# A new order for the opening of an attention + Fourier-mixing kernel, with query sums on VectorE and scaling ahead of the turn

## The chip, the cores and the metric

The kernel runs on one core of a Trainium2 chip. The metric is the device time of one execution in microseconds (us). A core has five engines that work side by side and wait for each other through semaphores: TensorE (PE in the profile; its weight loads are listed apart as PEld), VectorE (DVE), ScalarE (ACT), GpSimd (POOL) and SyncE (SP), which here only issues transfers. Each engine takes its own instructions strictly in the order in which the program issues them. A transfer (DMA) is issued by one of the engines' queues and then runs on its own.

## What is computed

```python
def _attn_ref(q, k, v):                      # q, k, v: (8 batches, 8 heads, 576 rows, 64)
    q_s = np.exp(q - np.max(q, axis=-1, keepdims=True))
    q_s = q_s / (np.sum(q_s, axis=-1, keepdims=True) + 1e-09)
    k_s = np.exp(k - np.max(k, axis=2, keepdims=True))
    k_s = k_s / (np.sum(k_s, axis=2, keepdims=True) + 1e-09)
    kv = np.einsum('bhsd,bhse->bhde', k_s, v)
    return np.einsum('bhsd,bhde->bhse', q_s, kv)

def _moe_ref(x, w_ch1, w_ch2):               # x: (8, 576, 512), the heads side by side
    X = np.fft.fft(np.fft.fft(x, axis=1), axis=2)
    u = x + np.real(X)
    mu, var = mean and variance of u over the last axis
    un = (u - mu) / np.sqrt(var + 1e-06)
    return u + np.maximum(un @ w_ch1, 0.0) @ w_ch2      # 512 x 2048 and 2048 x 512
```

All of it is float32. The two feed-forward weights arrive as 64-bit numbers and are turned into float32 on the chip, in part by steps called `c0 hi`, `c0 shift`, `c0 sign`, `c0 lo`, `c0 add` for the first block of columns.

## The kernel before

The eight batches go through three stages: attention, the two Fourier transforms with the layer normalisation, and the two feed-forward matmuls. Each batch has 576 rows: 512 of its own in four tiles of 128 and 64 that are left over. The left-over rows of batches 0 and 1 share one tile, called `t` here. A program of steps with times is written out in the kernel: every step is a pair (time, function), the main function sorts all pairs by time (the end of the printed code) and calls them in that order under `manual_schedule`. The times are labels for sorting. What counts is the order that results on each engine and the waits that data bring.

The change touches the opening: the work on batch 0 ahead of the first feed-forward matmul. Its steps and their order stand in the string `OPENING` (L86), and a few warm-up matmuls, which compute nothing that is used, in `WARM` (L85). `opening()` (L575) gives each name its function. The steps, in the order of the data:

- Loads. `loads_first()` (L246) gives the first transfers to SP's queue: four key tiles, the query tiles A and B in one transfer (`queries(0)`), half of the values (L285, L286), the query tiles C and D (`queries(1)`), the shared tile's four blocks of 32 rows (`shared()`, L271), the other half of the values, and then four single rows that take the first place in each of those four blocks (`shared_firsts()`, L274). A small exponential on ScalarE (`table`) has its function table loaded early.
- Keys. `k00` to `k03` are four tiles of the transposed keys of batch 0. `max` (VectorE, L529) finds the maximum of a row, `exp` (ScalarE) the exponential and its sum, `turn` and `four` transpose it on TensorE and copy it on ScalarE; `last` and `fifth` (L548) do the same for the left-over rows. `k0 inverse` (L550 to L552) inverts the sums, `k00 kv` to `k03 kv` multiply with the values, and `k0 scale0` and `k0 scale1` (L561) scale the result. The names with `k1` are the same for batch 1.
- Queries. A, B, C and D are the four tiles of batch 0: A is (column half 0, unit 0), B (1, 1), C (0, 1) and D (1, 0). `max` (VectorE, L805), `less` (GpSimd, L810; on VectorE for `t`) and `exp` (ScalarE, L814) make the exponential in place. `turn` and `copy` transpose it into a tile `qT` from a pool of two buffers (L832). `ones` (L876) multiplies the transposed tile with a matrix of ones, which gives the sum of each head; `inverse` (L887) inverts it on VectorE; `kv` (L884) multiplies with the keys-times-values, and `out` (L899) scales the product on its way from PSUM to the tile `x`. For `t` the sum, inverse and scaling come ahead of the turn (`t inverse`, `t normal`, on VectorE).
- Folding. `t turn`, `t copy`, `t fold`, `t join`, `t kv`, `t parts`, `t folds` bring the shared rows into the transform. `tokens0` to `tokens3` (L945) are sums and differences of pairs of outputs: 0 and 2 of A's with C's, 1 and 3 of D's with B's. `columns`, `by`, `again` (L951 to L965) fold the columns likewise. `b0` to `b4` (`block()`) are the transform along the columns; `m0` and `m1` (`mix_own()`, L1061) that along the rows, with the `sums` at L1042, for the column halves 0 and 1.
- Normalisation. `s00` to `s11` (L1075) are the statistics of the four mixed tiles, `root0` and `root1` the square roots (L1079), `normal` the normalised tile, `turn` (L1105) and `laid` (L1114) its transpose into the tile that the feed-forward reads.
- Feed-forward. The first matmul takes its first columns in two halves (`half(0)` and `half(1)`, L1169). `half(0)` reads the tiles 00 and 01 and `half(1)` the tiles 10 and 11. Next come the matmuls of L1160, which read the converted weights (L377).

Time `first = 46.9` (L1588) places the feed-forward in the list.

Of the kernel before, what the change touches and what calls it, by code (L numbers as in the profile page):

```python
# [46 lines left out]
P = 128  # L47
# [37 lines left out]
WARM = (3, 3), (24.7, 6), (41.9, 2), (43.45, 1), (44.5, 1)  # L85
OPENING = """  # L86
4.30 k00 max, 5.10 k00 exp, 5.50 k01 max, 6.05 k00 turn, 6.30 k01 exp, 6.65 k02 max, 7.06 k00 four,
7.25 k01 turn, 7.56 k02 exp, 7.75 k03 max, 8.32 k01 four, 8.51 k02 turn, 8.82 k03 exp, 8.90 A max, 9.50 B max,
9.58 k02 four, 9.65 A less, 9.77 k0 last, 10.10 k0 inverse, 10.27 k03 turn, 10.42 k0 fifth, 10.69 B less,
10.80 A exp, 11.20 k00 kv, 11.30 k03 four, 11.84 B exp, 11.85 A turn, 12.20 C max, 12.30 k01 kv, 12.45 A copy,  # L90
12.80 D max, 12.95 B turn, 12.95 C less, 13.40 A ones, 13.55 B copy, 13.99 D less, 14.10 C exp, 14.20 k02 kv,
14.35 A inverse, 14.85 C turn, 15.00 t max, 15.14 D exp, 15.30 k03 kv, 15.75 t less, 15.95 D turn,
16.35 k0 scale0, 16.40 B ones, 16.47 t exp, 16.80 k0 scale1, 17.14 t inverse, 17.25 B kv, 17.99 B inverse,
18.22 A kv, 18.35 C copy, 18.39 t normal, 19.01 B out, 19.19 t turn, 19.32 D copy, 19.63 k10 max, 19.69 C ones,
19.84 t copy, 20.30 A out, 20.43 k10 exp, 20.49 C kv, 20.92 C inverse, 21.39 t fold, 21.46 D ones,
22.09 t join, 22.26 D kv, 22.51 D inverse, 22.91 C out, 23.31 t kv, 23.53 D out, 24.15 tokens0, 24.21 k10 turn,
24.36 t parts, 24.77 tokens1, 25.39 columns0, 25.46 k10 four, 25.75 columns1, 26.23 by1, 26.59 by0,
26.80 c0 hi, 26.95 t folds, 27.45 c0 lo, 27.70 again0, 28.00 again1, 28.50 tokens3, 28.60 b0 times,
29.12 tokens2, 29.58 b1 times, 29.74 columns3, 29.80 b0 copies, 30.10 columns2, 30.56 b4 times, 30.58 by2,
30.78 b1 copies, 30.94 by3, 31.42 again2, 31.72 again3, 31.76 b4 copies, 32.22 k12 max, 32.32 b2 times,  # L100
32.89 c0 shift, 33.02 k12 exp, 33.30 b3 times, 33.59 c0 sign, 33.78 b2 copies, 34.19 k13 max, 34.28 k12 turn,
34.31 c0 add, 34.50 b3 copies, 34.86 k11 max, 35.05 k13 exp, 35.20 m0 times, 35.81 k12 four, 36.10 k13 turn,
36.31 m0 copy, 36.55 m1 times, 36.66 k11 exp, 36.81 m0 sums, 37.42 k13 four, 37.61 k1 last, 37.71 m0 add0,
37.92 m1 copy, 38.07 k11 turn, 38.27 k1 fifth, 38.39 m0 add1, 38.42 m1 sums, 38.77 k11 four, 38.92 k10 kv,
39.22 s00, 39.27 roots, 39.67 k11 kv, 39.69 m1 add1, 39.97 s01, 40.42 k12 kv, 40.87 root0, 40.99 m1 add0,
41.17 k13 kv, 41.67 scales0, 41.87 s11, 42.02 normal01, 42.62 s10, 42.77 turn01, 43.37 normal00, 43.52 root1,
43.87 scales1, 43.89 normal11, 43.95 laid01, 44.02 turn00, 44.22 normal10, 44.77 laid00, 44.87 turn10,
45.47 turn11, 45.62 laid10, 46.22 laid11, 53.00 k1 inverse, 53.30 k1 scale0, 53.60 k1 scale1"""
# [28 lines left out]
class _Block:  # L137
    def __init__(self, ctx, tc, q, kT, v, w1, w2, ft, cd, out):
# [38 lines left out]
        self.ones = c.tile([P, NR, H], F32, name="ones")  # L177
        nc.gpsimd.memset(self.ones[:], 0.0)
        for h in range(2):
            nc.gpsimd.memset(self.ones[64 * h:64 * h + 64].rearrange("p r h -> p (r h)")[:, h::H + 2], 1.0)  # L180

# [31 lines left out]
        self.unused = None  # L213
# [32 lines left out]
    def loads_first(self, fetch):  # L246
# [20 lines left out]
        def shared():  # L267
            flat = self.q[b:b + 2].rearrange("b s n -> (b s) n")
            for i in range(4):
                a = i * S // 2 + P  # L270
                load(tail[i * Q:(i + 1) * Q], flat[a:a + Q])  # L271

        def shared_firsts():
            load(tail[0:P:Q], self.q[b:b + 2].rearrange("b s n -> (b s) n")[::S // 2])  # L274
# [5 lines left out]
        def keys(r):  # L280
            load(ks[r], self.kT[b, r * P:(r + 1) * P, :])
# [10 lines left out]
        def second(r):  # L292
# [6 lines left out]
        order = [lambda: nc.gpsimd.memset(v[0:64, 4, :], 0.0), table, *(lambda r=r: keys(r) for r in range(NR)), lambda: queries(0),  # L299
                 lambda: values(0), lambda: queries(1), shared, lambda: values(2), shared_firsts, self.tables,  # L300
# [214 lines left out]
    def first_keys(self, b):  # L515
# [4 lines left out]
        copy, box, top = nc.vector.tensor_copy if b == 0 else nc.scalar.copy, {}, {}  # L520
# [26 lines left out]
        def fifth():  # L547
            copy(self.fifth[64:], box["last"][64:])  # L548
# [26 lines left out]
    def opening(self, fetch, converted):  # L575


        V, G = self.nc.vector, self.nc.gpsimd
# [14 lines left out]
        named("t max,t less,t exp", self.q_exp_spread(shared, V))  # L593
        named("t inverse,t normal", self.q_inverse(shared, V, V))
# [3 lines left out]
        for n, it in own.items():  # L598
            named(f"{n} max,{n} less,{n} exp", self.q_exp_spread(it))
            named(f"{n} turn,{n} copy", self.q_turn(it))  # L600
            named(f"{n} ones,{n} kv,{n} inverse,{n} out", self.q_times_kv(it))
# [12 lines left out]
        steps["roots"] = self.roots_next  # L614
        for i in range(1):
# [182 lines left out]
    def q_exp_spread(self, it, e=None):  # L798
# [885 lines left out]
```

## Time and profile before

| what | value |
|---|---|
| time, three runs | 1070.05, 1070.17, 1070.81 us; median 1070.17 |
| the profiled execution | 1070.52 us, of which the profile's span is 1068.70 us |
| TensorE busy | 1057.0 us (99% of the span) |
| TensorE weight loads (beside matmuls) | 921.2 us (86%) |
| VectorE busy | 699.5 us (65%) |
| ScalarE, GpSimd busy | 403.5 us (38%), 376.5 us (35%) |
| chain of work that ended last | TensorE 86%, VectorE 3%, ScalarE 2% |
| transfers | 236.04 MB, mean 221 GB/s |

The profile records one execution. A busy share is an average over the whole span. In the first of 40 slices of it (26.7 us each) TensorE is busy for eight tenths and VectorE for six tenths, and in the last slice TensorE for eight tenths; in the slices between them TensorE stands at nine tenths or more. The granted TensorE clock is at nine tenths or more in all slices. A line of a group names the source line (L1105), the engine, the operation, what it writes and reads with tile names, the shapes, how often, the busy time, the mean of one in nanoseconds, and the idle time of the engine just ahead with the work that ended it. A line of a timeline gives start and length in us and then the same, with the idle time in brackets. The chain of waits follows the work that ended last backwards, from each instruction to the one that released it.

### The profile page before, as it was taken

Reading aid. Unit: us, or ns where it says so; the run is one execution under the profiler, and the core shown is the slowest. Engines: PE = TensorE matmul, PEld = TensorE weight load, DVE = VectorE, ACT = ScalarE, POOL = GpSimd, SP = SyncE. Lnnn points to the kernel's source line nnn. Section 1 sums busy time; section 2 is a strip of 40 time slices with the busy share of each in tenths; the row PEclk is TensorE's granted clock in tenths of the full one; section 3 lists DMA queues with packets and bytes.
Section 4 is the critical chain, followed back from the end, with each engine's and each line's share of the span. In section 5 each row is a group of like instructions: output and inputs, shape, how many; then the busy total and the mean of one; then the engine's idle time right before and its main releaser. Section 6 shows DMA issues by size and latency. Waiting matters only on the chain.

```text
span 1068.7 us, 16982 instructions
## 1 busy us (share of the span) xinstructions
PE 1057.0 (99%) x6394; PEld 921.2 (86%) x6394; DVE 699.5 (65%) x1350; ACT 403.5 (38%) x953; POOL 376.5 (35%) x317
## 2 busy tenths in 40 slices
PE   8999999999999999999999999999999999999998
PEld 7744556988898899889988999889988998899897
DVE  6897887684455874677556765678457745674563
ACT  5675534632245215521453234521552132231210
POOL 3262220265412743454515542374336350000000
PEclk9999999999999999999999999999999999999999
DMA  8697478648976576645755576557644575576464
GB/s 278 225 305 244 174 247 295 210 161 281 337 258 209 180 254 233 226 176 202 269 181 193 197 247 223 187 196 257 223 167 158 201 253 178 197 257 223 170 220 145
DMA packets 113546, 236.04 MB, mean 221 GB/s; under 512 B 23272, under 2 KB 74856, under 8 KB 102840
## 3 DMA queue, kind: packets, MB, share of 16 engines
q1 hardware_dynamic: 113096, 234.42, 64.3%
q8 instruction: 51, 0.84, 0.3%
q10 hardware_dynamic: 288, 0.26, 0.1%
q14 instruction: 31, 0.25, 0.1%
q0 software_dynamic: 80, 0.26, 0.1%
HBM read 199.79 MB, written 39.06 MB: 223 GB/s over the span
## 4 chain that ended last, share of the span: by engine, by line
PE 86%; DVE 3%; ACT 2%; issue 0%; ACTq 0%; DVEq 0%
PE bb L1244 15%; PE bb L1371 10%; PE bc L1244 10%; PE ba L1244 10%; PE bc L1371 7%; PE ba L1371 7%; PE bb L1341 5%; PE acc L716 3%; PE acc L884 2%; PE bc L1181 2%; PE bb L1460 2%; PE acc L997 2%; PE acc L1000 2%; PE acc L1025 2%; PE bc L1460 1%; PE ba L1460 1%
## 5 line engine op out<-in xcount | busy, mean ns | idle before, releaser
L1244 PE MATMUL bb<-unT,big 128*128 128x256 f32 x768 | 184.4, 380 | 0.8 <-DVE u L1214 0.8
L1244 PEld LDWEIGHTS bb<-unT,big 128*128 128x128 f32 x768 | 142.5, 190 | 20.3 <-DVE u L1214 2.3
L1256 ACT ACTIVATE big<-big 128x512 f32<-128x512 f32 x96 | 60.4, 629 | 194.8 <-DVE big L1255 194.3
L1244 PE MATMUL ba<-unT,big 128*128 128x256 f32 x512 | 123.8, 379 | 0.0
L1244 PE MATMUL bc<-unT,big 128*128 128x256 f32 x512 | 123.5, 379 | 0.0
L1214 DVE TENSOR_TENSOR u<-bb,s 128x512 f32<-128x512 f32 x66 | 45.6, 690 | 105.9 <-PE bb L1244 83.0
L383 POOL TENSOR_TENSOR big<-big 128x512 f32<-128x512 f32 x24 | 30.5, 1269 | 226.6 <-ACT big L1256 226.6
L1244 PEld LDWEIGHTS bc<-unT,big 128*128 128x128 f32 x512 | 94.7, 190 | 12.5 <-DVE big L1255 1.0
L1371 PE MATMUL bb<-big 128*128 128x128 f32 x848 | 105.1, 275 | 0.3 <-DVE u L1378 0.3
L1244 PEld LDWEIGHTS ba<-unT,big 128*128 128x128 f32 x512 | 94.4, 190 | 12.2 <-issue 0.5
L1371 PEld LDWEIGHTS bb<-big 128*128 128x128 f32 x848 | 99.6, 192 | 0.5 <-DVE u L1378 0.4
L1321 POOL TENSOR_TENSOR x<-x,big 128x512 f32<-128x512 f32 x45 | 57.7, 1296 | 62.7 <-issue 32.9
L1371 PE MATMUL ba<-big 128*128 128x128 f32 x640 | 79.6, 275 | 0.0
L766 ACT ACTIVATE q<-q,qm 128x64 f32<-128x64 f32 x248 | 67.1, 338 | 31.2 <-DVE qm L760 24.7
L1371 PEld LDWEIGHTS ba<-big 128*128 128x128 f32 x640 | 76.3, 192 | 1.2
L1317 DVE TENSOR_TENSOR big<-big 128x512 f32<-128x512 f32 x98 | 76.3, 818 | 0.0
L1341 PE MATMUL bb<-big 128*128 128x256 f32 x256 | 58.7, 381 | 0.0
L1378 DVE TENSOR_TENSOR u<-bb,s 128x256 f32<-128x256 f32 x40 | 16.8, 421 | 63.9 <-PE bb L1371 60.6
L1255 DVE TENSOR_TENSOR big<-bc,u 128x512 f32<-128x512 f32 x64 | 44.0, 687 | 21.8 <-PE bc L1244 21.0
L1120 POOL TENSOR_TENSOR unT<-unT 128x512 f32<-128x512 f32 x8 | 14.2, 1771 | 123.0 <-DVE unT L1120 100.8
L1341 PEld LDWEIGHTS bb<-big 128*128 128x128 f32 x256 | 48.2, 190 | 8.0 <-DVE big L1255 1.1
L1371 PE MATMUL bc<-big 128*128 128x128 f32 x416 | 51.5, 275 | 0.0
(265 smaller groups left out, 2022.4 us busy)
## 6 DMA issues: line engine op xcount, KB each, us to landing
big<-w2d SPq DMA_DIRECT2D x67, 1024.0 KB, 4.8
big<-w1s SPq DMA_DIRECT2D x64, 896.0 KB, 4.9
big<-w2s SPq DMA_DIRECT2D x16, 1024.0 KB, 6.3
big<-in_w_dram SPq DMA_DIRECT2D x21, 512.0 KB, 6.4
w2d<-big SPq DMA_DIRECT2D x42, 256.0 KB, 5.4
q<-in_q_dram SPq DMA_DIRECT2D x28, 256.0 KB, 6.1
k<-in_kT_dram SPq DMA_DIRECT2D x24, 288.0 KB, 5.5
v<-in_v_dram SPq DMA_DIRECT2D x24, 256.0 KB, 4.7
```

The costliest lines, as they stand in the source:

```text
L383: e1.tensor_tensor(out=to(4), in0=at(2), in1=at(3), op=ALU.add)
L716: nc.tensor.matmul(pk, lhsT=ks[:, c, :], rhs=v[:, c, :], start=(c == 0), stop=(c == NC - 1))
L766: nc.scalar.activation(q[:, h, :], q[:, h, :], ACT.Exp, bias=m[:, h:h + 1])
L1214: plus = lambda t: V.tensor_tensor(out=temp(t), in0=box["bb"][:], in1=box["s1"][:], op=ALU.add)
L1244: nc.tensor.matmul(bank()[:, i, :], lhsT=w[:, WA_AT[m], k * P:(k + 1) * P], rhs=self.unT[g][:, B_AT[m], k, :], start=first and i == 0 and ...
L1255: steps = [(0, lambda: V.tensor_tensor(out=hp(i), in0=bank()[:], in1=u()[:], op=ALU.add)), (0.8, lambda: nc.scalar.activation(hp(i), hp(i) ...
L1256: (0.8, lambda: nc.scalar.activation(hp(i), hp(i), ACT.Relu))]
L1317: e.tensor_tensor(out=to(o), in0=to(x), in1=to(y), op=op)
L1321: E.tensor_tensor(out=x, in0=x, in1=tile(m), op=ALU.add)
L1341: nc.tensor.matmul(box[name][:, i, :], lhsT=h[p][:, A_AT[m], i * P:(i + 1) * P], rhs=self.stream[n][:, p, :], start=p == 0 and (m != 1 or ...
L1371: nc.tensor.matmul(box[place[n]][:, i, :], lhsT=own(m)(A_AT[n])[:, f, :], rhs=w[:, r // 2, r % 2 * P:r % 2 * P + P], start=first and f == ...
L1460: nc.tensor.matmul(bank()[:, i, :], lhsT=h[p][:, A_AT[m], i * P:(i + 1) * P], rhs=w[:, p, :], start=first and i == 0 and p == 0, stop=p == ...
```

## The change

It has five parts.

1. Sums and scaling of the queries. The tile `ones`, its 16 matmuls and the four inverses that follow are gone. Five steps `sum` on VectorE (`reduce_sum`, one for each of t, A, B, C, D) run on the exponentials before the turn. Two steps invert them together: `inverse1` those of t and C, `inverse2` those of D, A and B. The tiles t, C and D are scaled before the turn by GpSimd (`normal`). A and B are scaled by VectorE at `out` as before. The `out` of C and D is a plain copy on ScalarE.
2. Loads. The four block loads of `shared()` are issued by ScalarE's queue ahead of `table`. The load of the four first rows, `firsts`, is issued by ScalarE's queue after the second key exponential, no longer by SP.
3. Engines. `t less` goes from VectorE to GpSimd, `k0 fifth` from VectorE to ScalarE.
4. Places. For batch 0 `qT` has its own places in the weights' tile `w1sb`, where before two buffers took turns. The products of A, B and C go to named PSUM banks. The token sums read the products of C and D straight from PSUM.
5. Order. `OPENING` and `WARM` are new. The half `m1` is mixed before `m0`, and the tiles 11 and 10 are normalised, turned and laid before 01 and 00. `first` is 47.6. `half(0)` still reads 00 and 01.

```diff
-WARM = (3, 3), (24.7, 6), (41.9, 2), (43.45, 1), (44.5, 1)
+WARM = (3, 3), (24.33, 6), (41.46, 1), (44.02, 1)
 OPENING = """
...
+4.10 k00 max, 4.90 k00 exp, 5.25 k01 max, 5.90 k00 turn, 6.05 k01 exp, 6.07 firsts, 6.70 k02 max,
+7.00 k00 four, 7.05 k01 turn, 7.50 k02 exp, 7.75 k03 max, 8.37 k01 four, 8.50 k02 turn, 8.87 k03 exp,
+9.00 B max, 9.60 t max, 9.74 k02 four, 9.75 B less, 9.87 k0 last, 10.20 A max, 10.39 k03 turn, 10.57 k0 fifth,
+10.79 t less, 11.07 B exp, 11.22 k00 kv, 11.57 k03 four, 11.72 B sum, 11.83 A less, 12.07 t exp, 12.32 C max,
+12.34 B turn, 12.79 k01 kv, 12.92 t sum, 12.98 A exp, 13.07 C less, 13.48 B copy, 13.52 D max, 13.91 A turn,
+14.12 k0 inverse, 14.22 C exp, 14.36 k02 kv, 14.47 A sum, 14.47 D less, 14.72 A copy, 15.07 C sum, 15.62 D exp,
+15.71 k03 kv, 15.81 inverse1, 16.27 D sum, 16.31 t normal, 17.06 k0 scale0, 17.36 C normal, 17.46 t turn,
+17.56 k0 scale1, 18.06 B kv, 18.16 t copy, 18.41 inverse2, 18.81 t fold, 18.96 C turn, 19.41 A kv, 19.53 B out,
+19.53 D normal, 19.66 C copy, 20.15 k10 max, 20.34 C kv, 20.82 A out, 20.95 k10 exp, 21.24 D turn,
+21.58 t join, 21.94 D copy, 21.95 k10 turn, 22.13 tokens0, 22.55 k10 four, 22.62 D kv, 22.75 tokens2,
+23.05 C out, 23.37 columns0, 23.52 t kv, 23.77 D out, 23.77 tokens1, 24.39 tokens3, 24.57 t parts,
...
+34.35 k11 four, 34.47 m1 times, 34.85 k13 exp, 35.57 m0 times,
...
+41.24 k12 kv, 41.32 normal11, 41.85 s01, 42.36 turn11, 42.71 s00, 42.96 k13 kv, 43.57 normal10, 43.66 root0,
+44.07 scales0, 44.22 turn10, 44.27 laid11, 44.42 normal01, 44.89 normal00, 44.97 laid10, 45.17 turn01,
+45.77 turn00, 45.92 laid01, 46.52 laid00, 53.00 k1 inverse, 53.30 k1 scale0, 53.60 k1 scale1"""
...
             for i in range(4):
                 a = i * S // 2 + P
-                load(tail[i * Q:(i + 1) * Q], flat[a:a + Q])
-
-        def shared_firsts():
-            load(tail[0:P:Q], self.q[b:b + 2].rearrange("b s n -> (b s) n")[::S // 2])
+                nc.scalar.dma_start(tail[i * Q:(i + 1) * Q], flat[a:a + Q])
...
         def fifth():
-            copy(self.fifth[64:], box["last"][64:])
+            nc.scalar.copy(self.fifth[64:], box["last"][64:])
...
-        named("t max,t less,t exp", self.q_exp_spread(shared, V))
-        named("t inverse,t normal", self.q_inverse(shared, V, V))
+        named("t max,t less,t exp", self.q_exp_spread(shared))
+        sums = self.small.tile([P, 5, H], F32, tag="sums", name="sums", bufs=1)
+        firsts = {"t": shared, **{n: own[n] for n in "CDAB"}}
+        heads = {n: self.live[it][0].rearrange("p (h d) -> p h d", h=H) for n, it in firsts.items()}
+        spread = {n: sums[:, i].unsqueeze(2).to_broadcast([P, H, DH]) for i, n in enumerate(firsts)}
+        for i, n in enumerate(firsts):
+            steps[f"{n} sum"] = lambda i=i, n=n: V.reduce_sum(sums[:, i], heads[n], axis=AX.X)
+            if n in "tCD":
+                steps[f"{n} normal"] = lambda n=n: G.tensor_tensor(out=heads[n], in0=heads[n], in1=spread[n], op=ALU.mult)
+            else:
+                self.live[own[n]].append(spread[n])
+
+        def inverse(s):
+            V.tensor_scalar(out=sums[:, s], in0=sums[:, s], scalar1=ATT_EPS, scalar2=None, op0=ALU.add)
+            V.reciprocal(sums[:, s], sums[:, s])
+
+        for i, s in enumerate((slice(0, 2), slice(2, 5))):
+            steps[f"inverse{i + 1}"] = lambda s=s: inverse(s)
...
+        steps["firsts"] = lambda: nc.scalar.dma_start(self.at_start[3][0:P:Q], rows)
...
-            (e or nc.gpsimd).tensor_tensor(out=heads(), in0=heads(), in1=m, op=ALU.add)
+            nc.gpsimd.tensor_tensor(out=heads(), in0=heads(), in1=m, op=ALU.add)
...
-            qT = self.work.tile([P, NR, P], F32, tag="qT", name="qT", bufs=2)
-            self.nc.scalar.copy(qT[:], pt[:] if c == u else pt[:, :, ::-1])
+            if b == 0:
+                qT = self.w1sb[:, 1 + c + 2 * u, :].rearrange("p (r n) -> p r n", n=P)
+            else:
+                qT = self.work.tile([P, NR, P], F32, tag="qT", name="qT", bufs=2)[:]
+            self.nc.scalar.copy(qT, pt[:] if c == u else pt[:, :, ::-1])
...
-        return [(0, ones), (0, times), (1, inverse), (1.3, out)] if b == 0 else [(0, times), (1.3, out)]
+        return [(0, times), (1.3, out)]
...
-                e.tensor_tensor(out=eo[i][:, 0:D], in0=self.xpart(b, i % 2, 0), in1=self.xpart(b, i % 2, 1), op=op)
+                x, y = ((self.px.get((i % 2, u)) if b == 0 else None) for u in range(2))
+                x, y = (self.xpart(b, i % 2, u) if z is None else z for u, z in enumerate((x, y)))
+                e.tensor_tensor(out=eo[i][:, 0:D], in0=x, in1=y, op=op)
...
-    first, second, both = 46.9, 56, 77
+    first, second, both = 47.6, 56, 77
```

In the changed program the lines are shifted: the query maxima are at L815, `less` at L820, the sums at L591, the scalings of t, C and D at L593, the token sums at L953, the mixed sums at L1050, the turn of the normalised tiles at L1113 and the halves of the first feed-forward matmul at L1177.

## The prediction

> **What bounds the kernel now.** I read the busy time by stretches first, then TensorE's waits after the opening, then the timelines. Columns of the first: stretch in us, its length, busy time of PE, PEld, DVE, ACT and POOL, clock, DMA share, GB/s.
>
> ```profile
> 12.00:16.00 4.00, 3.79 (x35) 3.71 (x34) 1.81 (x5) 2.33 (x4) 2.04 (x2) 1.00 0.59 128
> 16.00:30.00 14.00, 13.02 (x104) 12.19 (x103) 12.82 (x35) 5.89 (x11) 1.48 (x3) 1.00 1.03 344
> ...
> 48.80:1068.70 1019.90, 1014.00 (x6092) 883.21 (x6090) 662.91 (x1260) 375.09 (x888) 361.93 (x282) 1.00 0.64 218
> ```
>
> From 48.8 us on, TensorE is busy 1014.00 of 1019.90 us, and all its waits there come to 1.3 us:
>
> ```profile
> PE bb L1244 <- DVE u L1214: 0.8, 2, 0.4
> PE bb L1371 <- DVE u L1378: 0.3, 1, 0.3
> PE bb L1160 <- POOL big L377: 0.2, 1, 0.2
> ```
>
> So the end is the start of the first feed-forward matmul (L1169, `half(0)`) plus a fixed queue of TensorE work. The changed program issues the same TensorE, ScalarE, GpSimd and SP instructions in the same order after the opening; on VectorE one instruction shifts among its neighbours. The change can only move that start, and the small wait of L1160 behind it. TensorE's timeline there, and what feeds the chain in front (start, length, work, what ended the idle time):
>
> ```profile
> 47.91 1.09 PE L1105 MATMUL tr<-ident,eo 128*128 128x128 f32 x8
> 48.84 3.62 PE L1169 MATMUL ba<-unT,big 128*128 128x256 f32 x16
> 52.65 3.70 PE L1160 MATMUL bb<-unT,big 128*128 128x512 f32 x8 [0.20 <-POOL big L377]
> ```
> ```profile
> 8.46 1.28 DVE L805 TENSOR_REDUCE qm<-big 128x8 f32<-128x512 f32 x2 [0.45 <-DMA big<-in_q_dram]
> 9.65 0.70 DVE L551 TENSOR_SCALAR kinv<-kinv 128x4 f32<-128x4 f32 x1
> 12.39 1.28 DVE L805 TENSOR_REDUCE qm<-big 128x8 f32<-128x512 f32 x2 [1.10 <-DMA big<-in_q_dram]
> ...
> 15.84 0.69 DVE L805 TENSOR_REDUCE qm<-big 128x8 f32<-128x512 f32 x1 [0.76 <-DMA big<-in_q_dram]
> ...
> 25.77 1.28 DVE L945 TENSOR_TENSOR eo<-x 128x512 f32<-128x512 f32 x2
> ```
> ```profile
> 9.29 2.04 POOL L810 TENSOR_TENSOR big<-big,qm 128x512 f32<-128x512 f32 x2 [3.99 <-DVE qm L805]
> 13.16 2.04 POOL L810 TENSOR_TENSOR big<-big,qm 128x512 f32<-128x512 f32 x2 [1.83 <-DVE qm L805]
> ```
> ```profile
> 5.05 2.42 SPq L271 DMA_DIRECT2D big<-in_q_dram  x4
> 8.45 0.38 SPq L285 DMA_DIRECT2D big<-in_v_dram  x1
> 10.09 0.49 SPq L286 DMA_DIRECT2D big<-in_v_dram  x1
> 13.78 0.62 SPq L274 DMA_DIRECT2D big<-in_q_dram  x1
> ```
>
> The opening hangs on two arrivals: queries C and D (read at 12.39) and the shared rows (read at 15.84). From 17.81 to 38 us VectorE has no idle gap, so it sets the pace to the token sums at 25.77 and beyond. SP holds the four-row load (L274) until the block rows have landed, and everything behind it with it: that is the stretch at 128 GB/s.
>
> [...] L551 took 0.70 us from 9.65, to the end of GpSimd's first L810 at 10.33, where the same form (L784) took 0.17. [...] Before's longest gap in mid-opening, 1.68 us, left transposes at 0.11 us each; the new order has none above 1.3, so I charge nothing.
>
> **The change part by part.** I laid the trace's durations along both orders, each engine in order, each wait to the end of what it waits for, 0.05 us for a handover. For before this puts `half(0)` at 48.54 (trace: 48.84), so I read differences only.
>
> *Loads.* The four block loads (4 x 64 KB) go from the middle of SP's list to ScalarE's queue at the start. Their issues (SP's cost 0.4 to 0.7 us) take some 2 us of ScalarE ahead of the 1.28 us table load: ready at about 4.2, and the first exponential waits for its maximum, about 4.9, anyway: 0. The 256 KB now come ahead of C/D; at the mean 310 GB/s of the first 40 us that is 0.83 us, so C/D arrive at 12.39 + 0.83 = 13.2. Bounds: 12.39 (they fill slack) and 13.65 (when SP saw the block rows land, with the same bytes in front). I take 13.2. Keys and A/B shift by the same 0.5 to 0.8; these have slack. The four-row load, behind the second exponential, costs ScalarE about 0.5 (SP paid 0.62) and lands near 8.6 (before: issued 13.78, read 15.84). It may be as late as 11.3 before VectorE's `t max`, ahead of `A max`, holds anything up. SP no longer stands from 10.6 to 13.8. The tables, second keys and words come some 1.5 us sooner; no step on the path waits for them: 0.
>
> *Sums.* Sixteen `ones` matmuls (0.2 us each, 3.2 in all) and four inverses on VectorE (0.17 + 0.20 each) go, with the shared tile's subtraction (0.69) and scaling (0.64) on VectorE. Five reductions of 0.69 us come (the shared one was there: net +2.76), and two inverses of 0.4. GpSimd gets one subtraction and three scalings: 4 x 1.04 = 4.2 us by L810; its other 128x512 sums run 1.27 to 1.77. I take 1.04, since the work beside it is reductions, reads of PSUM and small operations. VectorE loses two of four scaled evictions (-1.35; ScalarE copies C and D at 0.58 each instead) and the 0.70 copy `k0 fifth`. C's and D's sums read PSUM directly; L899 (PSUM) took 0.675 and L945 0.684, so that is free.
>
> *The path after.* C's maximum starts 13.25, its subtraction 13.98; D's 15.20; C's exponential 15.07, D's 16.29; the sums of C and D start 16.01 and 17.05; the scaling of keys-times-values runs 17.66 to 18.48 (before 17.81 to 18.67). The inverse of t and C ends 17.1; GpSimd scales t to 18.2, C to 19.2, adds for T, then scales D to 21.4. Then D's turn, copy (22.8) and matmul, its ScalarE copy at 24.7, and the token sums that read it start at 25.3. The first pair started at 22.45, so VectorE has already done two sums and one fold, but waits 1.29 for D. The first block's operands are ready at about 30.0 and the blocks go on unbroken: first mixed sums at 37.2 (before 38.81), first statistics 39.5 (41.52), a lead of 1.6 to 2.0. Behind them the lead shrinks to 1.4 (second root 44.4 against 45.78).
>
> *The last turn gives some back.* `half(0)` needs tiles 00 and 01. Before they were laid first and the turns of 10 and 11 ran straight into it. Now they come last: after the turn of 00, VectorE's 0.69 us copy stands alone on TensorE's path, about 0.8 with handovers. `half(0)` lands at 47.92, 0.62 earlier than 48.54. The conversion awaited by L1160 starts with this copy, so its 0.15 to 0.2 wait goes as well: in all -0.77.
>
> Sum: profiled before 1070.52 = span 1068.70 + 1.82 around it; after 1070.52 - 0.77 = 1069.75. The shown median, 1070.17, is 0.35 below the profiled run, hence 1069.4.
>
> **Rivals.**
> 1. *Nothing left* (chance 0.20): C/D come at 13.65 (0.41 of the gain) and GpSimd's additions for T meet VectorE's (+0.2), or GpSimd's eight passes average 1.24. For: L856 has run at 0.56 on average, against 0.47 here. Net 0: 1070.2.
> 2. *GpSimd becomes the opening's bound* (0.11), the slower case: eight serial passes, the last three between the sums and the D turn. Up to about 1.24 us each the gain survives; from there every 0.1 costs over 0.5. At 1.56 (L1317's and L945's rows) the same walk gives +3.1: 1073.3. Against: the four L810 passes differ by 2 ns, with VectorE at reductions beside them, and the new neighbours are of that kind.
> 3. *The loads were the real brake* (0.09): with the hole gone (4 us at 344 - 128 GB/s, 0.86 MB or 2.5 us of transfer) C/D and the values come early and the opening gains 2.3: 1067.9. Against: C/D lie in front of the hole, and with no delay to them at all the walk gives -1.3.
>
> **How the numbers follow.** Forecast -0.77 has 0.60. Its own range is from C/D unshifted (-1.3, 1068.9) to rival 1. What a measurement can tell from no change is 0.2%, 2.1 us. Faster by more: rival 3, 0.09. Slower by more: rival 2, 0.11. The rest, 0.80, within. The range 1067.9 to 1071.2 reaches to rival 3's value, and above to GpSimd at about 1.35 us (+1.0); beyond it lie most of rival 2 and a half of rival 3, under 2 in 10.
>
> **What would show it.** Right: C's maximum near 13.2, no SP gap behind the value loads, GpSimd's scalings (L593) at 1.04, token sums waiting about 1 us for D, first mixed sums 1.6 us earlier, a TensorE gap of about 1 us in front of the first feed-forward matmul, and that matmul 0.3 to 1.2 us earlier than 48.84. Wrong: L593 or L820 above 1.25, the four-row load read after 11.3, C's maximum after 14, or transposes at 0.2 us late in the opening.

## The result, and the profile after

| | before | after |
|---|---|---|
| median (7 runs each) | 1070.17 us (1070.05 to 1070.94) | 1073.72 us (1071.97 to 1074.62) |
| profiled execution, span | 1070.52, 1068.70 | 1073.72, 1072.0 |
| ratio, 95% interval | | 1.0029 (1.0019 to 1.0038) |

The change costs 3.5 us by the medians (3.2 us in the profiled executions) where 0.8 us of gain was forecast, and the time lies outside the range. First the windows of the changed kernel, with the columns of the prediction:

```profile
12.00:16.00 4.00, 4.00 (x31) 3.78 (x30) 2.33 (x4) 2.69 (x5) 1.57 (x2) 1.00 1.06 356
16.00:30.00 14.00, 12.07 (x94) 11.14 (x93) 12.74 (x30) 9.05 (x18) 7.14 (x9) 1.00 1.11 340
50.60:1072.00 1021.40, 1014.13 (x6090) 883.09 (x6090) 662.69 (x1259) 374.33 (x886) 361.79 (x282) 1.00 0.64 218
```

The transfers do run without the hole now (356 GB/s from 12 to 16 us, where 128 stood). Yet the last stretch shows two losses: it begins at 50.6 and not at 48.8, and it is 1.5 us longer (1021.4 against 1019.9) with the same TensorE work (1014.13 against 1014.00). TensorE's timeline at the first feed-forward matmul, and all that TensorE waits for behind 48 us:

```profile
48.67 1.12 PE L1113 MATMUL tr<-ident,eo 128*128 128x128 f32 x8 [0.39 <-ACT eo L1107]
50.67 3.69 PE L1177 MATMUL ba<-unT,big 128*128 128x256 f32 x16 [0.88 <-DVE unT L1122]
```

```profile
PE acc L897 <- ACT qT L845: 1.1, 1, 1.1
PE tr L1113 <- ACT eo L1107: 0.9, 2, 0.5
PE ba L1177 <- DVE unT L1122: 0.9, 1, 0.9
PE bb L1252 <- DVE u L1222: 0.8, 2, 0.4
PE tr L1113 <- ACT unT L1122: 0.5, 1, 0.5
```

`half(0)` starts at 50.67 (48.84 before): 1.83 later. Behind it two waits are new: 1.1 us for batch 1's transposed queries (L897, at 113 us) and about 1 us in two pieces at batch 1's normalised tiles (L1113, at 165 and 170 us). In the kernel before neither was there. I read four points in each trace: `half(0)`, the second product of batch 1 (P), batch 1's first turn (T) and the end.

| | half(0) | half(0) to P | P to T | T to end | end |
|---|---|---|---|---|---|
| before | 48.84 | 61.75 | 51.91 | 906.24 | 1068.74 |
| after | 50.67 | 62.48 | 52.58 | 906.22 | 1071.95 |
| difference | 1.83 | 0.73 | 0.67 | -0.02 | 3.21 |

Three losses have to be explained, one for each of the first three columns. The first shows on VectorE and ScalarE early in the opening:

```profile
9.31 0.69 DVE L815 TENSOR_REDUCE qm<-big 128x8 f32<-128x512 f32 x1 [0.72 <-DMA big<-in_q_dram]
13.67 1.28 DVE L815 TENSOR_REDUCE qm<-big 128x8 f32<-128x512 f32 x2 [3.67 <-DMA big<-in_q_dram]
...
15.46 0.68 DVE L815 TENSOR_REDUCE qm<-big 128x8 f32<-128x512 f32 x1
...
39.54 0.76 DVE L1050 TENSOR_TENSOR eo<-acc,sn 128x256 f32<-128x256 f32 x2 [1.19 <-ACT sn L1042]
```

```profile
8.03 1.19 ACTq L624 DMA_DIRECT2D big<-in_q_dram  x1
9.26 0.59 ACT L532 COPY ks<-tr 128x512 f32<-128x512 f32 x1 [2.04 <-DMA big<-in_q_dram]
9.74 0.78 ACT L524 ACTIVATE big<-big,km 128x576 f32<-128x576 f32 x1
```

VectorE takes `B max` at 9.31 and then stands 3.67 us in front of `t max`, until the four rows have landed (13.64); `A max` (the second of the two at 13.67, though A's rows came with B's), `C max` (15.46) and all else are behind it. ScalarE stands 2.04 us: it comes to the four-row load (L624) at 7.2, waits to 8.03 for the blocks, which these rows overwrite in part, and takes 1.19 to issue it. `k00 four` and the third key exponential are behind it.

### The profile page after: what moved, and what is told of

Its sections match the earlier page's. It is cut to its first block, busy times and chain, and to the rows that moved or that the text cites. A ratio compares the mean times of both kernels' runs of the same rounds, so it can differ in the third digit from the quotient of the medians.

```text
span 1072.0 us, 16912 instructions
## 1 busy us (share of the span) xinstructions
PE 1054.5 (98%) x6358; PEld 917.9 (86%) x6358; DVE 698.8 (65%) x1343; ACT 405.4 (38%) x956; POOL 380.3 (35%) x318
## 4 chain that ended last, share of the span: by engine, by line
PE 84%; DVE 3%; ACT 2%; DMA 1%; issue 0%; ACTq 0%; DVEq 0%
PE bb L1252 15%; PE bb L1379 10%; PE bc L1252 10%; PE ba L1252 10%; PE bc L1379 7%; PE ba L1379 6%; PE bb L1349 5%; PE acc L726 2%; PE acc L897 2%; PE bb L1468 2%; PE acc L1005 2%; PE acc L1008 2%; PE bc L1189 2%; PE acc L1033 1%; PE bc L1468 1%; PE ba L1468 1%
```

## The experiments

Each is timed against the kernel before on the same chip (its median there 1070.5 to 1070.9). Times to the end of a step come from the profiled execution, a single run, whose own time can be one or two microseconds off the median.

### The four-row load

**rows_first**, the rows ahead of everything:

```diff
+            nc.scalar.dma_start(tail[0:P:Q], flat[::S // 2])
             for i in range(4):
                 a = i * S // 2 + P
-                nc.scalar.dma_start(tail[i * Q:(i + 1) * Q], flat[a:a + Q])
+                nc.scalar.dma_start(tail[i * Q + 1:(i + 1) * Q], flat[a + 1:a + Q])
```

> The changed kernel, with the four-row load issued first of all on ScalarE's queue; the four block loads then bring 31 rows each, so that they need not be ordered against it. The opening order is unchanged, apart from the removed step. Theory R (the four rows, which landed at 13.6 us, hold VectorE in front of `t max`, and with it the whole opening): `t max` at about 10, no 3.7 us gap on VectorE, half(0) at about 48.3 us where the changed kernel has 50.67, so 2.3 us less; time about 1070.4 to 1071.2. Rival S (the opening is late because C and D, and the keys, come later behind 256 KB more): half(0) stays above 50, time within 0.5 us of the changed kernel.

Measured 1082.50 us, 1.0105 (1.0089 to 1.0120), `half(0)` at 60.98. It tells nothing of the two theories, since it brought a delay of its own. In the trace's packets the 124 rows of the 31-row loads start one after the other, about every 0.125 us, from 5.60 to 21.14 us; the 128 rows of the 32-row loads of the changed kernel are through from 2.28 to 7.2. SP's loads from the values to the tables were issued from 9.12 to 21.84 us meanwhile, in the changed kernel from 4.58 to 9.30; what held SP between them was not shown:

```profile
3.66 0.39 SPq L283 DMA_DIRECT2D big<-in_q_dram  x1
9.12 0.38 SPq L278 DMA_DIRECT2D big<-in_v_dram  x1
9.54 0.59 SPq L279 DMA_DIRECT2D big<-in_v_dram  x1
13.26 0.37 SPq L283 DMA_DIRECT2D big<-in_q_dram  x1
```

**t_later**, VectorE's order alone (the four steps of t moved):

```diff
-9.60 t max ... 10.79 t less ... 12.07 t exp ... 12.92 t sum
+13.30 t max ... 13.55 t less ... 14.90 t exp ... 15.30 t sum
```

> The changed kernel with the steps of t (max, subtraction, exponential, sum) moved behind those of A and C; the loads as in the changed kernel. Theory R, in the form that it is VectorE's place in the order that hurts: `A max` at about 10, half(0) at about 49.0, 1.6 us less than the changed kernel's 50.67. Rival theory H (ScalarE is held for 2 us by the issue of the four-row load, 0.8 waiting for the blocks and 1.2 issuing, and this delays the key turns): half(0) stays at 50 or later, since ScalarE is held here too.

Measured 1074.25, 1.0031 (1.0019 to 1.0043), `half(0)` at 50.48. The 3.67 us in front of `t max` are gone, but VectorE stands 3.09 us at `B sum` instead, for B's exponential, which ScalarE gives late. So moving t is not enough. H passes this test, R alone doesn't.

**rows_sp**, ScalarE's hold alone (the load goes to SP behind the value loads), and **rows_sp_t**, both:

```diff
-nc.scalar.dma_start(self.at_start[3][0:P:Q], rows)     # behind k01 exp
+load(tail[0:P:Q], flat[::S // 2])                      # SP, behind values(2)
```

> The changed kernel with the four-row load alone put back on SP's queue, behind the value loads, where the blocks have landed by the time SP comes to it. The block loads stay on ScalarE's queue, the order stays. Theory H (ScalarE, held 2 us at this load, is what delays the opening): ScalarE's gap of 2 us between the second and third key exponential goes, half(0) falls from 50.7 to about 48.5, time about 1071.5. Theory R (VectorE waits at `t max` for the rows, which land no sooner from SP, about 13.6): the gap of 3.7 us on VectorE stays, half(0) stays at 50.3 to 50.7, time 1073.5.

> The same, with the steps of t (max, subtraction, exponential, sum) behind those of A and C as well. Theory RH (each of the two waits is enough to hold the opening at 50, and the gain shows only when both are gone): half(0) at about 48.6, 2 us less than the changed kernel, with no wait above 1.5 us on VectorE between 9 and 16 us; time about 1071.5 to 1072.0. If neither wait is the cause (C, D and the keys' arrival is): half(0) stays above 50.

Measured 1075.30, 1.0043 (1.0026 to 1.0059), and 1073.26, 1.0025 (1.0015 to 1.0035); `half(0)` at 52.29 and 50.69. In rows_sp ScalarE's gap goes and VectorE's stays (4.38 us), as R says, and H's 48.5 failed. It is even slower than the changed kernel: `t max` starts 0.36 later there, and TensorE, which stands for 3.73 us until 17.55, is slow afterwards (1.91 us for eight matmuls that take 1.06; granted clock 0.68 from 16 to 21 us). In rows_sp_t no gap of VectorE between 9 and 16 is above 1.5, and still nothing is won: my expectation of 48.6 failed. The trace shows why: a TensorE gap of 3.05 us in front of the turn of t, and slow matmuls a little behind it (1.92 us for eight at 21.64). The next pair tests this.

**mended** and **mended_warm**. mended is rows_sp_t with the k1 steps 0.7 later (see below) and `half(1)` ahead of `half(0)` (what is first and last on their shared tile changes with it); mended_warm adds one entry:

```diff
-        first[0] = [(-0.9, lambda: half(0)), (0, lambda: half(1)), (2.5, lambda: relu(0))]
+        first[0] = [(-0.9, lambda: half(1)), (0, lambda: half(0)), (2.5, lambda: relu(0))]
...
```
```diff
-WARM = (3, 3), (24.33, 6), (41.46, 1), (44.02, 1)
+WARM = (3, 3), (16.6, 6), (24.33, 6), (41.46, 1), (44.02, 1)
```

> All mends on the changed kernel: the four rows on SP, t behind A and C, the k1 steps 0.7 later, and the first feed-forward matmul in the other order, half(1) first, which reads the tiles 11 and 10 that are laid first. By the theories R, H and K, and by the prediction's step that the last turn gives back about 0.8 us: the first half starts at about 47.6, the gap of 0.9 us in front of it goes, the wait at 113 us goes; against before about 1.2 us less, 1069.7. If the wait in front of the halves isn't set by the last tile laid: the first half starts no earlier than in rows_sp_t.

> The kernel `mended` with six warm-up matmuls in TensorE's gap ahead of the turn of t. Theory C (in `mended` the gap of 2 us and the waits around it slowed TensorE's clock, so that eight 128x128 matmuls at 20.57 took 1.92 us where others take 1.06): those matmuls take 1.06 again, the first half comes 0.8 to 1.3 us sooner than 50.11, time about 1070.6. If the matmuls' length has another cause: no change.

Measured 1071.51, 1.0007 (1.0000 to 1.0014), and 1070.78, 1.0003 (0.9994 to 1.0012). mended missed the 1069.7 that I expected, and 47.6 for its first half. The same eight matmuls in mended and in mended_warm:

```profile
19.89 0.89 PE L833 MATMUL tr<-ident,big 128*128 128x128 f32 x4 [1.96 <-POOL big L596]
20.57 1.92 PE L898 MATMUL bc<-kvr,big 128*128 128x128 f32 x8
```

```profile
16.53 2.75 PE L236 MATMUL ba<-kvr,ident 128*128 128x256 f32 x12
19.67 0.66 PE L833 MATMUL tr<-ident,big 128*128 128x128 f32 x4 [0.38 <-POOL big L596]
20.16 1.06 PE L898 MATMUL bc<-kvr,big 128*128 128x128 f32 x8
```

And the windows over them, columns as before (the granted clock is the third from the end), of mended, of two parts of the same time in mended, and of mended_warm:

```profile
19.80:24.00 4.20, 4.11 (x22) 4.11 (x23) 3.75 (x8) 1.21 (x3) 2.95 (x5) 0.59 1.12 329
```

```profile
16.80:20.10 3.30, 1.34 (x13) 1.15 (x12) 3.19 (x9) 0.68 (x2) 1.66 (x3) 1.00 1.13 331
20.20:23.50 3.30, 3.30 (x18) 3.30 (x16) 3.00 (x7) 0.71 (x2) 2.55 (x4) 0.50 1.14 328
```

```profile
19.60:24.00 4.40, 4.26 (x36) 4.02 (x36) 4.30 (x10) 1.71 (x3) 2.93 (x5) 1.00 1.12 333
```

With the gap filled the clock stays at 1.00, the matmuls take 1.06 us and not 1.92, and the first half starts at 48.66 and not at 50.11. Of these 1.45 us some 1.2 are the clock's: the first half starts 35.76 us after `t max` in mended and 34.53 in mended_warm, and the other 0.2 is an earlier landing of the four rows. In both the gap in front of the halves (0.88 in the changed kernel) is gone. The wait ahead of the slow matmuls was 1.96 us in mended, 3.05 in rows_sp_t and 3.73 in rows_sp.

In mended TensorE was busy for 1.34 of the 3.30 us from 16.80 to 20.10, still at clock 1.00, and the clock was 0.50 over the next 3.30 us, in which it was busy throughout. From 24.00 to 26.00 us it was 1.00 again. In rows_sp_t the mean was 0.70 from 19.40 to 25.00 us and 1.00 from 25.00 to 31.00. Whether the single wait slows the clock or how little TensorE does over a longer stretch, these runs don't show.

**no_rows**, the case that the prediction had assumed: neither effect of the four rows. The kernel leaves the load out, so four rows of the shared tile hold other data.

```diff
-6.05 k01 exp, 6.07 firsts, 6.70 k02 max
+6.05 k01 exp, 6.70 k02 max
```

> The changed kernel without the load of the four first rows (the shared tile keeps four rows that it should not, so four rows of each of the two batches' shared part come out of other data; all the work and its order stay). ScalarE isn't held and the shared tile is whole when its blocks have landed, at about 8. This is the case that the prediction took for granted. Theory T (the four rows, in both their effects, are the whole loss ahead of half(0)): VectorE goes through `t max` at about 10 without the 3.7 us gap, no 2 us gap on ScalarE, half(0) at 47.6 to 48.3, 2.4 to 3 us earlier than in the changed kernel; time about 1070.3 with the k1 steps as they are. If half(0) stays above 49.5, the opening's order is slow for another reason, such as GpSimd's passes or TensorE's clock.

Measured 1071.08, 1.0005 (0.9996 to 1.0014). VectorE's and TensorE's lines:

```profile
9.02 1.87 DVE L813 TENSOR_REDUCE qm<-big 128x8 f32<-128x512 f32 x3 [0.54 <-DMA big<-in_q_dram]
...
36.47 0.76 DVE L1048 TENSOR_TENSOR eo<-acc,sn 128x256 f32<-128x256 f32 x2 [1.19 <-ACT sn L1040]
```

```profile
47.60 3.69 PE L1175 MATMUL ba<-unT,big 128*128 128x256 f32 x16 [0.88 <-DVE unT L1120]
```

The three maxima run without a gap, `half(0)` comes at 47.60, 3.07 us earlier than in the changed kernel and 1.24 earlier than before. The first loss is settled: it is the four-row load. Its size follows the landing: with the four rows in place, three traces of the same order (the changed kernel, k1_later and after_fetch, both below) have `t max` at 13.67, 13.05 and 12.53, and `half(0)` 37.0 us later in all three. The line of k1_later:

```profile
13.05 1.28 DVE L815 TENSOR_REDUCE qm<-big 128x8 f32<-128x512 f32 x2 [3.51 <-DMA big<-in_q_dram]
```

And yet the kernel is no faster than before: the whole lead of 1.24 us is lost behind `half(0)`.

**before_loads** and **before_loads_sp**: the new loads in the kernel before, first with the four rows on ScalarE behind `k01 exp`, then with them kept on SP.

> The kernel before with the changed loads alone: block loads first on ScalarE's queue, the four-row load on ScalarE's queue behind the second key exponential. The order of everything else is that of before, where `t max` stands behind `D max`. Theory R: the four rows land at about 13.6, ahead of where `t max` stands, so VectorE doesn't wait for them; but ScalarE is held about 2 us at the issue and the keys' turns shift; half(0) about 49.6 to 49.9 (48.84 before), time about 1071.3. Theory that the loads were the brake (rival 3 of the prediction): faster than before by 1 us or more.

> The kernel before with the block loads first on ScalarE's queue, and the four-row load kept on SP behind the value loads: the loads of before_loads without ScalarE's hold. Theory H: the loss of before_loads (2.2 us against before) goes, half(0) at about 49.0, time 1070.9 or up to 0.3 less, as the four rows land before `t max`. Theory that the 256 KB ahead of keys and queries cost it: half(0) stays above 50 and time at 1072.5 or more.

Measured 1073.13, 1.0020 (1.0013 to 1.0028), and 1070.48, 1.0002 (0.9993 to 1.0011); `half(0)` at 51.19 and 50.16. The second is 1.2 later than I expected, in a profiled execution (1071.64) that is as much above its median. In the order of before, where `t max` stands late, ScalarE's hold alone costs 2 us of the total, and the early block loads show neither a cost nor a gain.

### Behind half(0): the k1 steps

In the changed kernel `first` moved by 0.7 while the k1 steps kept their times, so they passed a sign step (L364) of the weights' conversion. VectorE's timeline:

```profile
56.88 0.68 DVE L361 TENSOR_SCALAR big<-acc 128x512 int32<-128x512 int32 x1
57.48 0.94 DVE L543 TENSOR_SCALAR kinv<-kinv 128x4 f32<-128x4 f32 x1
58.46 0.18 DVE L544 RECIPROCAL kinv<-kinv 128x4 f32<-128x4 f32 x1
58.67 0.42 DVE L555 TENSOR_TENSOR kvr<-acc,kinv 64x256 f32<-64x256 f32 x1
59.02 0.67 DVE L364 SCALAR_TENSOR_TENSOR big<-acc,big 128x512 int32<-128x512 int32 x1
```

The sign step starts 2.14 us after the shift (L361) where it started 0.72 us after it in before, and L543 takes 0.94 us (0.22 before) while GpSimd's L369 runs beside it until 58.40.

```diff
-53.00 k1 inverse, 53.30 k1 scale0, 53.60 k1 scale1
+53.70 k1 inverse, 54.00 k1 scale0, 54.30 k1 scale1
```

This is **k1_later** on the changed kernel and **no_rows_k1** on no_rows; **before_k1** moves them the other way, to 52.30, in the kernel before.

> The changed kernel with the three steps `k1 inverse`, `k1 scale0`, `k1 scale1` 0.7 later in the list, as `first` was moved, so that VectorE has the order of the kernel before again: both sign steps ahead of the inverse. Theory K (behind half(0) the conversion chain lost another 0.7 to 0.9 us to the inverse and scaling that stand ahead of a sign step): half(0) unchanged at 50.7, TensorE's wait of 1.1 us for batch 1's qT at 113 us falls to about 0.2 to 0.5, time about 0.7 lower, 1073.0. Rival N (that part is variation in the landing of stores around 150 us): no change, 1073.7, and the wait of 1.1 us stays.

> The same with the k1 steps 0.7 later, so that both sign steps stand ahead of them as in the kernel before. Theory K: 0.5 to 0.9 us less than no_rows, by a smaller wait for batch 1's qT at 113 us; about 1069.6, where the prediction put the changed kernel. Rival N: equal to no_rows.

> The kernel before with the three k1 steps 0.7 earlier, which gives VectorE the order of the changed kernel there: the inverse and the first scaling ahead of a sign step. Theory K, in reverse and on the kernel with the narrower spread: half(0) unchanged at about 48.8, a wait of 0.5 to 1 us for batch 1's qT appears, time 0.5 to 0.9 us above before. Rival N: no change.

Measured 1072.11, 1.0012 (1.0006 to 1.0019); 1070.24, 1.0000 (0.9991 to 1.0009); 1071.15, 1.0004 (0.9998 to 1.0011). The way from `half(0)` to P: 61.69 against 62.48 in the changed kernel, 61.47 against 62.80 in no_rows, 62.76 against 61.75 in before, where a wait appears that wasn't there:

```profile
PE acc L884 <- ACT qT L832: 1.1, 1, 1.1
```

All three agree in sign with K and are of its size, though before_k1's interval of the time still touches 1. The times of no_rows and no_rows_k1 overlap too. (k1_later's `half(0)`, 50.04, came 0.6 earlier than in the changed kernel, since the four rows happened to land that much earlier; so of its 1.6 us less I count 0.8.) Over all seventeen traces VectorE's part is the same: the third shift starts 9.5 us behind `half(0)` in the eight with the k1 steps early, and 8.8 to 8.9 in the nine with them late. What reaches P is mixed with other causes: 61.84 to 62.80 (mean 62.4) against 61.47 to 62.74 (mean 61.9).

### Behind half(0): a fetch of instructions

The last loss is the way from P to T. It is 51.91 us (51.90 once) in all four kernels with the opening of before and 52.28 to 53.01 in all ten with the new one, whatever else they have. At 150 us VectorE waits to overwrite a tile (`spare`) that a store still reads, in after and in before:

```profile
154.54 0.43 DVE L419 TENSOR_TENSOR spare<-big 128x256 f32<-128x256 f32 x1 [3.52 <-DMA w2s<-spare]
```

```profile
150.85 0.42 DVE L427 TENSOR_TENSOR spare<-big 128x256 f32<-128x256 f32 x1 [2.41 <-DMA w2s<-spare]
```

The wait is 1.1 us longer, and batch 1's statistics stand behind it. SP issues that store at the same place in both. The DMA queues of the changed kernel between 144 and 156 us hold something that before's do not:

```profile
q1 hardware_dynamic: 2875, 3.68, 94.0%
q8 instruction: 1, 0.02, 0.7%
```

One packet of 16 KB of instructions. From the trace's packets and completion events (that store reports in sixteen parts):

```
                     16 KB fetch     store w2s<-spare lands: 15th part   16th part
before                  135.80                            150.78          150.83
after                   149.23 (1.26 us)                  153.50          154.51
no_rows                 148.95 (0.94 us)                  151.09          152.04
mended_warm             142.52 (1.04 us)                  150.27          152.12
```

In the three kernels with the later fetch the sixteenth part came 0.95 to 1.85 us behind the fifteenth, in before 0.05. I read from these figures that the fetch, at 0.94 to 1.26 us, holds up one of the 16 parts of what is queued behind it. There are 50 such fetches (51 before), 0.8 MB. I take them for TensorE's stream (an estimate): where TensorE matmuls alone were added, in after_fetch below, the one at 149.23 moved to 137.5. The new opening has 18 TensorE matmuls fewer in the program ahead of `half(0)`, so the fetch that stood at 135.8 comes later and meets the burst of loads and stores from 142 to 155 us.

**after_fetch**, **no_rows_fetch** (on no_rows_k1) and **mended_fetch** (on mended_warm) move the fetch, with more and narrower warm-up matmuls ahead of `half(0)`:

```diff
-        for _ in range(n):
-            self.nc.tensor.matmul(t[:, 0:2 * P], lhsT=self.ident[:], rhs=self.kvr[1][:, 0:2, :], start=True, stop=True)
+        for _ in range(2 * n):
+            self.nc.tensor.matmul(t[:, 0:P], lhsT=self.ident[:], rhs=self.kvr[1][:, 0, :], start=True, stop=True)
-WARM = (3, 3), (24.33, 6), (41.46, 1), (44.02, 1)
+WARM = (3, 4), (8.45, 2), (24.33, 6), (41.46, 1), (44.02, 1)
```

> The changed kernel with its warm-up matmuls cut into twice as many of half the width, and a few more in gaps of TensorE: 28 matmuls of 128 columns in place of 11 of 256, so some 70 TensorE instructions more ahead of the first feed-forward matmul. Nothing else moves. Theory F (a fetch of 16 KB of TensorE's instructions, at 149.2 us in the changed kernel and at 135.8 in the kernel before, falls into the burst of loads and stores at 142 to 155 us and makes one of the 16 DMA engines 1 us late, for which VectorE waits): the fetch moves to about 138, the sixteenth part of the stores lands within 0.3 us of the fifteenth, the way from the second batch-1 product to the first turn of batch 1 falls from 52.6 to 51.9 us as in the kernel before, time 0.9 to 1.2 us less, about 1072.6. Rival V (the store's landing varies by itself): the 52.6 stays, time 1073.7.

> The kernel no_rows_k1 (no load of the four first rows, k1 steps 0.7 later) with the same cut of the warm-up matmuls. Theory F: the fetch moves from 148 to about 136, the way from the second batch-1 product to the first turn falls from 52.8 to 51.9, half(0) stays near 47.8, time 0.9 to 1.2 us less than no_rows_k1, about 1069.2. Rival V: equal to no_rows_k1, 1070.2.

> The kernel mended_warm with the cut of the warm-up matmuls, which computes the whole. By theory F the fetch leaves the burst (142.5 us before), the way from the second batch-1 product to the first turn falls from 52.8 to 51.9, time 0.9 us less than mended_warm: about 1069.9, a little under the kernel before. Rival V: 1070.8.

Measured 1072.10, 1.0013 (1.0006 to 1.0020); 1069.45, 0.9986 (0.9979 to 0.9992); 1070.04, 0.9992 (0.9983 to 1.0000). The fetch is at 137.5, 136.2 and 136.4, the sixteenth part lands within 0.2 us of the fifteenth, P to T is 51.91 in all three, and VectorE's wait in after_fetch is back to before's:

```profile
151.90 0.42 DVE L419 TENSOR_TENSOR spare<-big 128x256 f32<-128x256 f32 x1 [2.34 <-DMA w2s<-spare]
```

Theory F is shown, and not by these three alone: in the ten kernels with the late fetch the sixteenth part lands 0.86 to 1.85 us behind the fifteenth, in the other seven 0.17 or less. Of after_fetch's 1.6 us less, 0.67 is this. Its `half(0)` also comes 1.1 earlier (49.55), and that is the four rows, which landed so much sooner in this execution:

```profile
12.53 1.28 DVE L815 TENSOR_REDUCE qm<-big 128x8 f32<-128x512 f32 x2 [2.58 <-DMA big<-in_q_dram]
```

From T to the end after_fetch and no_rows_fetch take 906.63 and 906.79, about half a microsecond more than the others; why is open. no_rows_fetch shows the effect a second time: its next fetch stands at 71.24, a load of weights at that place lands with its last part 1.2 us late (76.25, the fifteenth 75.04), and from `half(0)` to P it takes 62.74 although its k1 steps are late.

mended_fetch computes the whole and is the best of the complete ones: level with the kernel before (0.9992, with an interval up to 1.0000), where the changed kernel stands at 1.0029. In its profiled execution, the slowest of 13, the four rows come 0.7 later than in mended_warm (`t max` at 14.84 and 14.13), and its first half with them (49.37, in both 34.53 after `t max`). Their landing still sets the opening.

## Why the prediction was wrong

**The step that failed first** is the four-row load: "costs ScalarE about 0.5 (SP paid 0.62) and lands near 8.6". It held ScalarE for 2.04 us and landed at 13.64, and `half(0)` came 3.07 us later than without it (no_rows). Two things were left out. The rows overwrite part of the blocks, and the issue waited for the blocks on either queue: 3.0 us on SP in before, to 8.03 on ScalarE in the changed kernel. The prediction had read this in SP's line ("SP holds the four-row load (L274) until the block rows have landed") and then priced the same load on ScalarE without it. And 8 KB were priced at before's 2 us from issue to landing, though the rows now stood behind C and D: issued by 9.21, their packets ran from 12.62, right behind C's and D's landing (12.57). The text named a landing after 11.3 as what would make it wrong, and gave it no chance. No run tests that threshold; by the 37.0 us from `t max` to `half(0)`, no_rows' 47.60 belongs to a `t max` at 10.6 (an estimate), so it was somewhat generous.

**The second** is "the end is the start of the first feed-forward matmul (L1169, `half(0)`) plus a fixed queue of TensorE work". It was read from TensorE having next to no waits behind 48.8 us. That showed that nothing was late, not how little it would take: in before, the copy that P needs ended at 110.53 and P started at 110.59.

```profile
109.95 0.58 ACT L832 COPY qT<-tr 128x512 f32<-128x512 f32 x1
...
110.59 1.16 PE L884 MATMUL acc<-kvr,qT 128*128 128x128 f32 x8
```

no_rows had its `half(0)` 1.24 us ahead of before and ended 0.7 later.

**The third** is "on VectorE one instruction shifts among its neighbours", at no cost. The changed kernel lost 0.73 there (k1_later won 0.79 back), since its neighbours carry the conversion that TensorE waits for at P, and since L543 took 0.94 us, to the end of GpSimd's pass (0.22 in before). The prediction had measured the like in before (L551, 0.70 us) and applied it to that one instruction only. (Its comparison there is of 128x4 with 128x8 elements; the same 128x4 took 0.16 us in the changed kernel at 17.36, so the reading stands.) In the opening `inverse2` was longer as well: L598 took 0.62 us, to 21.62, beside a GpSimd scaling to 21.58, and 0.87 in no_rows; the L598 of `inverse1`, at 18.93 with no pass beside it, took 0.17.

**Missing altogether** was the fetch, 0.67. What the prediction said of TensorE's gaps ("none above 1.3, so I charge nothing") was true of neither the changed kernel (2.28 at 10.66) nor its mends, and in mended the slow clock behind a wait of 1.96 cost some 1.2 us. In the changed kernel the slow clock cost nothing that shows: its record has TensorE at full clock only from 13.5 us on (7.0 in before; four transposes took 1.12 us at 12.45 and 0.60 at 14.55), after_fetch's from 7.5 on, and both have `half(0)` 37.0 us after `t max`.

**Right** were: C and D, inside their bounds (expected 13.2, bound from 12.39; landed 12.57); the sums (0.68 each); GpSimd's scalings,

```profile
19.54 2.04 POOL L593 TENSOR_TENSOR big<-big,sums 128x512 f32<-128x512 f32 x2 [0.97 <-DVE sums L599]
```

about 1.04 each, which ends rival 2, the slower case that was named; the wait for D, which came but was shorter (0.81, expected 1.29); and the last turn, which gives back 0.88 (expected 0.8). With the rows out of the way the walk along the order holds. no_rows has its first mixed sums at 36.47 (expected 37.2) and `half(0)` at 47.60, 1.24 ahead of before; C and D landed at 12.41 there, as early as before, and for that case the walk gave 1.3. That no_rows_fetch ends at 1069.45, where the prediction had put the change (1069.4), is in part luck. It does without the four rows, the way from `half(0)` to P still has about 1 us of loss in its trace, and against the kernel before on its own chip it is 1.3 us faster, where 0.77 was forecast. Slower was the outcome of a mechanism that none of the rivals had.

## What to carry to other kernels

A load that overwrites part of another load kept its wait here on either queue (3.0 us on SP, 0.8 on ScalarE), and its packets ran behind the bytes issued ahead of it (issued by 9.21, run from 12.62), so price the issue with the wait and the landing with those bytes. A start that comes sooner is worth nothing until the next waits behind it are known with their slack; where the trace shows no wait, look how long each input had been ready. And with 18 matmuls fewer a fetch of instructions came at 149.23 us and no longer at 135.80, in a busy stretch of DMA, and cost 0.67: look at the instruction queue when a part of the kernel that nobody touched is a microsecond late.

## What the runs showed of the hardware

- In the ten kernels that fetched 16 KB of instructions in the burst of transfers ahead of 155 us (at 159.4 in rows_first, where all is later), the last of the sixteen parts of a 512 KB store landed 0.86 to 1.85 us behind the fifteenth. In the seven that had fetched earlier it was 0.17 us or less. One such fetch took 0.94 to 1.26 us in the three traces of the table.
- Loads of 31 rows of 2 KB ran row after row, 124 rows in 15.5 us (rows_first); loads of 32 rows ran several rows at a time, 128 rows in 4.9 us (the changed kernel).
- Waits of 1.96, 3.05 and 3.73 us on TensorE (mended, rows_sp_t, rows_sp) were followed, at once or within 1.5 us, by a stretch at a lower granted clock: 0.50 from 20.20 to 23.50 us in mended, 0.70 on the mean from 19.40 to 25.00 in rows_sp_t, 0.68 from 16 to 21 in rows_sp. Eight matmuls that take 1.06 us took 1.91 to 1.92 there.
- Three small VectorE operations with a scalar ended with the GpSimd pass beside them: L543 of the changed kernel took 0.94 us, to 58.43 (the pass of 1.30 to 58.40), its L598 0.62, to 21.62 (21.58), and L551 of the kernel before 0.70, to 10.35 (10.33). Where the pass ended soon, at 56.50, L551 took 0.22, and L598 at 18.93, with no pass beside it, 0.17.
